# Attention into a gated MLP on one core: the order of work in the first six head pairs, the order of the weight loads, and the queue of the last stores

## The chip, the cores and the metric

The kernel runs on one core of a Trainium2 chip. A core has five engines with a queue each, which work on their own and meet only at semaphores: TensorE (PE in the profile; PEld is its loading of weights), VectorE (DVE), ScalarE (ACT), GpSimd (POOL) and SyncE (SP, which here only issues transfers). Each engine takes its instructions in the order in which the program issues them. The metric is device time in microseconds (us), lower is better. Before the change it is 472.25 us, the median of three runs from 472.16 to 472.7.

## The reference

The inputs are q, k and v of 8 batches, 12 heads, 448 positions and 64 columns, and two weight matrices. All is float32.

```python
scores = scale * np.matmul(q, k.transpose(0, 1, 3, 2))
m = np.max(scores, axis=-1, keepdims=True)
e = np.exp(scores - m)
attn = e / (np.sum(e, axis=-1, keepdims=True) + np.exp(-m) + 1e-09)
out = np.matmul(attn, v)          # -> x: (batch * position, head * column) = (3584, 768)
h = x @ w_in                      # (768, 2048)
g = h * np.tanh(np.where(h > 20.0, h, np.log1p(np.exp(np.minimum(h, 20.0)))))
result = g @ w_out                # (2048, 768) -> (3584, 768)
```

The scale is 1/8. The softmax has one more term in its denominator, exp(-m), and the activation g is Mish.

## The kernel before, in words

**Pairs.** Two heads of a batch are worked on together, as a pair; there are 48 pairs, six to a batch (`HP`), numbered p from 0. Of a pair, q, k and v are loaded by SP (line 144), cast to bf16 by POOL (lines 188, 194 and 174; pair 0 by DVE and ACT), and q and k are turned on PE by eight small transposes into one bank of PSUM (`transpose_pair`, line 211). `evac_qk` copies them from there to SBUF: q times the scale, and k, each 448 columns. In the first pairs both copies are ACT's (`act=True`, lines 242 and 252), later q is DVE's and k is ACT's. A bank for these transposes comes from a pool of two (`mo_take`), which is shared with two other uses below and is given back by the copy.

**Half steps.** A pair has four half steps s. I write (p, s). In s = 0, 1, 2 the scores of 128 rows of both heads are made by two matmuls (lines 282 and 285), in s = 3 the last 64 rows of both (lines 297 and 300). For each half step DVE takes the negated row maxima (line 308, 896 columns at once for s below 3, 448 for s = 3), and ACT the exponentials with their row sums (line 319, two instructions of 448 columns for s below 3, one for s = 3). After (p, 3) ACT also takes the exponential of the maxima (line 326). Three sets of banks hold scores, so the scores run three half steps ahead of the exponentials: `scores_ahead` issues the next ones as soon as `exps` has let a set go.

**Denominators and normalising.** `denominators` (lines 332 and 336) and `normalise` work on the pair before: a copy of the reciprocals (344), then seven multiplications, four on POOL (line 352) and three on DVE (354). The weights e are then turned. For pairs 0, 1 and 3 this is one transposing DMA from SP (line 358). For the others (`BY_PE`) it is four times seven transposes on PE (line 369), each followed by a copy of 896 columns on DVE (line 373). `av_pair` then makes the attention output, eight matmuls (line 391), and a copy to xT (line 400). These copies are put into a list, `late`, and issued by `flush_late` in the next half step, behind its exponentials; so they stand in the queue of their engine from that place on, whether or not the matmuls have come.

**The head of the program.** Before the loop, pairs 0 to 2 are loaded and pairs 0 and 1 turned. The loop over p from 0 to 5 (`HEAD`) and s from 0 to 3 then issues, in each half step: the exponentials of (p, s); in s = 1 the copies of q and k of pair p + 2; the late copies; the next scores; and in s = 0 the loads of pair p + 4, the denominators and the normalising of pair p - 1, the transposes of pair p + 2, the casts of pair p + 3 and some pieces of the weights. Three tables place the rest:

```python
TURN_HEAD = {(3, 2): [(2, 0)], (3, 3): [(2, 1)], (4, 0): [(2, 2)], (4, 1): [(2, 3)], ...}
AV_HEAD = {(3, 3): 0, (4, 2): 2, (4, 3): 1}
W_HEAD = {0: 3, 1: 1, 3: 1, 4: 1}
```

The first says at which half step which quarter of which pair's weights is turned on PE, the second where the attention outputs of pairs 0, 2 and 1 are made, the third how many pieces of weights are loaded for which p.

**The rest.** Units of three pairs follow. A unit u has twelve half steps, with matmuls of the layers as filler, and then eight groups of six matmuls of the first layer (line 414) with their Mish on ACT (line 420), each with its part of the work between units: denominators, normalising (for a unit's third pair wholly on POOL), transposes of the next pairs. The first unit in this form is u = 2, with pairs 6 to 8; pair 8 is still turned and copied inside its half steps, by DVE alone. Its first line 414 is the first large matmul of the program: it needs the outputs of pairs 0 to 5. The second layer (line 480) fills the half steps from u = 4 on. The weights come in 20 pieces, twelve of the first matrix and eight of the second, each one DMA from POOL (line 170). Six are loaded in the head, and `W_AT` and a line in the groups of u = 2 (718) place the others by half step.

**The end.** A block of 128 output rows is copied by DVE (line 467) and stored from SP (line 445), in as many parts as it crosses segments of 112 rows. The last block is stored in three column ranges, each in two parts of 112 and 16 rows.

Of the kernel before, what the change touches and what calls it, by code (L numbers as in the profile page):

```python
# [19 lines left out]
def kernel(  # L20
# [91 lines left out]
    GROUP_FROM = 2 * HP  # L112
    TURN_BY_DMA = (N_PAIRS - UNIT_PAIRS, N_PAIRS - UNIT_PAIRS + 1)
    q_rests = [
# [61 lines left out]
    def cast_pair(p, with_v=True):  # L176
# [10 lines left out]
        if p not in TURN_BY_DMA:  # L187
            cast_q(out=q_bf, in_=q_f.rearrange(by_t, t=NT))  # L188
        else:
            nc.gpsimd.tensor_scalar(  # L190
                out=q_bf, in0=q_f.rearrange(by_t, t=NT),
                scalar1=SCALE, scalar2=1.0, op0=ALU.mult, op1=ALU.mult,
            )
# [5 lines left out]
    def transpose_pair(p, bank=None):  # L199
# [16 lines left out]
        own = [] if bank is not None else [ps, ps_k] if p == 0 else [ps]  # L216
        qkT[p] = (by_s, own)

    def turn_by_dma(p):
        pair = [qk_pool.tile([128, S], BF16, tag=t, name=t) for t in ("qT", "kT")]  # L220
# [12 lines left out]
    def evac_qk(p, act=False):  # L233
        if p >= N_PAIRS:
            return
        (q_ps, k_ps), own = qkT[p]
        mo_free.extend(own)
        qT = qk_pool.tile([128, S], BF16, tag="qT", name="qT")
        kT = qk_pool.tile([128, S], BF16, tag="kT", name="kT")
        qkT[p] = (qT, kT)  # L240
# [193 lines left out]
    def store_rows(g, i, o_sb, cols):  # L434
# [6 lines left out]
        for r, n in sorted(parts, key=lambda part: -part[1]):  # L441
# [3 lines left out]
            nc.sync.dma_start(  # L445
# [126 lines left out]
    AV_HEAD = {(3, 3): 0, (4, 2): 2, (4, 3): 1}  # L572
# [3 lines left out]
    W_AT = ({5: 1, 9: 1}, {1: 1, 4: 1, 5: 1, 7: 1, 9: 1, 11: 1}, {3: 1, 5: 1, 7: 1, 9: 1})  # L576
# [15 lines left out]
    for p in range(HEAD):  # L592
        for s in range(STEPS):
# [20 lines left out]
            if (p, s) in AV_HEAD:  # L614
                av_pair(AV_HEAD[p, s], act=True)
# [3 lines left out]
    for u in range(UNITS_PER_B, N_UNITS + 2 * UNITS_PER_B):  # L619
# [86 lines left out]
        for f in range(FF_U):  # L706
# [11 lines left out]
            if u == UNITS_PER_B and f in (2, 6):  # L718
                load_w(1)
# [61 lines left out]
```

## Time and profile before

| | |
|---|---|
| median of three runs | 472.25 us |
| the profiled execution | 471.56 us |
| its span, first to last instruction | 469.7 us |
| busy PE / DVE / ACT / POOL | 93% / 72% / 73% / 40% of the span |
| first line 414 (first large matmul) | 63.61 us |
| last copy to the output buffer ends | 466.58 us |

The profile shows one execution. Its rows are groups of instructions by line, or single ones in order of time. In a row of the timeline stand the start, the duration, the engine, the line, the operation, output and input with their shapes, and in brackets how long the engine was idle before and what released it. PE's matmuls overlap in its pipeline, so that a row's duration is longer than its spacing from the next, and the same holds for ACT's and DVE's in small measure. A table by windows gives each engine's busy time in a stretch, the clock granted to TensorE as a share of the full one (PEclk), and the busy share of the transfer engines.

### The profile page before, as it was taken

How to read it: one execution, taken by the hardware profiler on the slowest of the kernel's cores; microseconds unless marked ns; L12 is line 12 of the kernel's file. 1: busy time of each engine (PE TensorE's matmuls, PEld its weight loads, DVE VectorE, ACT ScalarE, POOL GpSimd, SP SyncE). 2: the span in 40 equal slices, each digit the busy share in tenths (PEclk: the TensorE clock that was granted, in tenths of full speed). 3: DMA queues.
4: the chain of work that ended last, by engine and by line, in shares of the span. 5: the costliest groups of instructions: out<-in, count | busy, mean ns of one | idle time of the engine just before them, and what ended most of it. 6: DMA issues, size and time to landing. Idle time of an engine off the chain costs nothing.

```text
span 469.7 us, 8871 instructions
## 1 busy us (share of the span) xinstructions
PE 435.9 (93%) x3032; PEld 234.8 (50%) x3032; DVE 336.6 (72%) x727; ACT 344.2 (73%) x917; POOL 188.4 (40%) x358
## 2 busy tenths in 40 slices
PE   4565887899998999999999999999999999999996
PEld 2233544454544454555555454645455555555565
DVE  4788987968785897879787878788787978430121
ACT  5979787869796888979696969788797969312300
POOL 4876808364605354453636163435445360000000
PEclk9999698899999999999999999999999999999999
DMA  8999959999999989899999989998989995960213
GB/s 225 227 246 202 248 84 239 187 169 201 217 217 265 212 206 209 242 192 276 174 241 222 235 151 249 219 224 223 195 246 198 253 191 123 179 142 1 68 35 101
DMA packets 204300, 90.81 MB, mean 193 GB/s; under 512 B 160992, under 2 KB 200800, under 8 KB 204256
## 3 DMA queue, kind: packets, MB, share of 16 engines
q1 hardware_dynamic: 196768, 83.97, 82.5%
q0 software_dynamic: 7488, 6.29, 8.9%
q8 instruction: 23, 0.38, 0.3%
q14 instruction: 21, 0.17, 0.1%
HBM read 45.61 MB, written 11.01 MB: 121 GB/s over the span
## 4 chain that ended last, share of the span: by engine, by line
PE 79%; DVE 7%; ACT 7%; DMA 3%; issue 2%; POOL 2%; SPq 0%; DVEq 0%; ACTq 0%; POOLq 0%
PE mo L480 30%; PE mo L414 23%; PE b L391 6%; PE b L414 6%; ACT en L319 5%; DVE negm L308 5%; PE b L282 3%; PE sc L282 3%; PE sc L211 2%; PE mo L369 2%; PE b L211 1%; PE mo L290 1%; DMA q_f<-in_q_dram 1%; DMA w_in_sb<-in_moe_w_in_dram 1%; DMA k_f<-in_k_dram 1%
## 5 line engine op out<-in xcount | busy, mean ns | idle before, releaser
L480 PE MATMUL mo<-w_out_sb,gT 128*128 128x384 bf16 (+1 forms) x896 | 141.5, 304 | 0.7 <-DVE o_sb L467 0.7
L414 PE MATMUL mo<-xT,w_in_sb 128*128 128x448 bf16 x594 | 124.3, 352 | 1.2 <-DVE xT L400 0.6
L480 PEld LDWEIGHTS <-gT 128*128 128x128 bf16 x896 | 80.2, 98 | 58.5 <-issue 19.8
L420 ACT ACTIVATE gT<-mo 128x448 bf16<-128x448 f32 x99 | 53.7, 544 | 71.8 <-PE mo L414 71.5
L319 ACT ACTIVATE en<-sc,negm 128x448 bf16<-128x448 f32 x156 | 97.8, 641 | 11.5 <-DVE negm L308 8.2
L414 PEld LDWEIGHTS <-w_in_sb 128*128 128x128 bf16 x768 | 71.7, 98 | 65.6 <-issue 7.5
L308 DVE TENSOR_REDUCE negm<-b 128x1 f32<-128x448 f32 x144 | 79.7, 616 | 22.7 <-PE b L285 22.7
L308 DVE TENSOR_REDUCE negm<-sc 128x2 f32<-128x896 f32 x84 | 84.3, 1015 | 11.2 <-PE sc L285 4.0
L319 ACT ACTIVATE en<-b,negm 128x448 bf16<-128x448 f32 x144 | 89.5, 651 | 0.0
L352 POOL TENSOR_SCALAR en<-en,rden 128x448 bf16<-128x448 bf16 x115 | 71.8, 642 | 36.0 <-DVE rden L344 28.6
L188 POOL CAST q_bf<-q_f 112x512 bf16<-112x512 f32 x45 | 27.6, 614 | 105.1 <-DMA q_f<-in_q_dram 104.5
L467 DVE COPY o_sb<-mo 128x384 f32<-128x384 f32 (+1 forms) x64 | 32.2, 503 | 49.1 <-PE mo L480 45.3
L354 DVE TENSOR_SCALAR en<-en,rden 128x448 bf16<-128x448 bf16 x221 | 65.2, 363 | 0.5
L282 PE MATMUL sc<-kT,qT 64*128 64x448 bf16 x72 | 29.5, 418 | 12.7 <-ACT en L319 11.2
L414 PE MATMUL b<-xT,w_in_sb 128*128 128x448 bf16 x168 | 36.5, 352 | 0.0
L391 PE MATMUL b<-eT,v_bf 112*64 112x448 bf16 x304 | 35.8, 357 | 0.0
L319 ACT ACTIVATION_READ_ACCUMULATOR en<-sc,negm 128x1 f32 x156 | 33.0, 212 | 0.0
L319 ACT ACTIVATION_READ_ACCUMULATOR en<-b,negm 128x1 f32 x144 | 32.5, 226 | 0.0
L174 POOL CAST v_bf<-v_f 112x512 bf16<-112x512 f32 x48 | 29.7, 618 | 6.4 <-DMA v_f<-in_v_dram 5.9
L194 POOL CAST k_bf<-k_f 112x512 bf16<-112x512 f32 x47 | 28.8, 613 | 4.2 <-DMA k_f<-in_k_dram 3.7
L285 PE MATMUL sc<-kT,qT 64*128 64x448 bf16 x72 | 29.8, 422 | 0.0
L391 PEld LDWEIGHTS <-v_bf 112*64 112x64 bf16 x384 | 19.6, 111 | 19.0 <-issue 12.1
(67 smaller groups left out, 478.3 us busy)
## 6 DMA issues: line engine op xcount, KB each, us to landing
q_f<-in_q_dram SPq DMA_DIRECT2D x48, 224.0 KB, 4.7
k_f<-in_k_dram SPq DMA_DIRECT2D x48, 224.0 KB, 5.0
v_f<-in_v_dram SPq DMA_DIRECT2D x48, 224.0 KB, 5.1
w_in_sb<-in_moe_w_in_dram POOLq DMA_DIRECT2D x12, 256.0 KB, 6.1
w_out_sb<-in_moe_w_out_dram POOLq DMA_DIRECT2D x8, 384.0 KB, 6.7
out_dram<-o_sb SPq DMA_DIRECT2D x7, 336.0 KB, 3.3
out_dram<-o_sb SPq DMA_DIRECT2D x8, 288.0 KB, 4.2
out_dram<-o_sb SPq DMA_DIRECT2D x8, 240.0 KB, 3.5
```

Source lines behind the costliest of these rows:

```text
L174: nc.gpsimd.tensor_copy(out=casted[p][2], in_=loaded.pop(p)[2])
L282: nc.tensor.matmul(sc[0][:, 0:S], lhsT=qT[0:64, qa : qa + 128], rhs=kA, start=True, stop=True)
L285: nc.tensor.matmul(sc[1][:, 0:S], lhsT=qT[64:128, qb : qb + 128], rhs=kB, start=True, stop=True)
L308: nc.vector.tensor_reduce(out=negm, in_=scored, axis=AX.X, op=ALU.max, negate=True)
L319: nc.scalar.activation(out=st["en"][:, :, c, 0:SP_], in_=sc[bk][:, 0:S].rearrange("q (j c) -> q j c", j=NT), func=AF.Exp, bias=st["negm"][ ...
L352: nc.gpsimd.tensor_scalar(scalar2=1.0, op0=ALU.mult, op1=ALU.mult, **args)
L354: nc.vector.tensor_scalar(scalar2=None, op0=ALU.mult, **args)
L391: nc.tensor.matmul(av[h * 64 : (h + 1) * 64, 0:S], lhsT=v_bf[:, h, j * D : (j + 1) * D], rhs=e_h, start=(j == 0), stop=(j == NT - 1),)
L414: nc.tensor.matmul(h_ps[:, 0:S], lhsT=w_in_sb[:, dm, ff * 128 : (ff + 1) * 128], rhs=xT[b][:, dm, :], start=(dm == 0), stop=(dm == DM_T - 1),)
L420: nc.scalar.activation(out=gT[b][:, ff, :], in_=h_ps[:, 0:S], func=AF.Mish)
L467: nc.vector.tensor_copy(out=o_sb[:, cols], in_=st["o"][:, 0:n_cols])
L480: nc.tensor.matmul(st["o"][:, 0:n_cols], lhsT=src[:, ff, c0 : c0 + 128], rhs=w_out_sb[:, ff, cols], start=(ff == 0), stop=(ff == FF_T - 1),)
```

## The change

It has five parts.

1. For pairs 1 to 8 (`ONE_COPY`) POOL multiplies q by the scale in its cast, a multiplication in place of a copy, and q and k are copied from PSUM by one instruction of 896 columns, on ACT or, for pair 8, on DVE. The two buffers for q and k become one with two halves, for all pairs.
2. In the head, denominators and normalising of pair p - 1 are issued ahead of the scores of the half step instead of behind them, for p = 1 to 5, and the transposes of pair p + 2 too, for p = 1 to 4 (`TURN_FIRST`).
3. The attention output of pair 0 is made in (3, 1) instead of (3, 3). Its copy and that of pair 1 stay on ACT; pair 2's goes to DVE.
4. In the groups of u = 2 three pieces of weights are issued in the third group, instead of one there and one in the seventh. In the next unit the last place loads two pieces instead of one, and in the unit after two of four places fall away.
5. The smaller part of each of the last three stores is issued from ACT's queue.

```diff
+    ONE_COPY = range(1, HP + UNIT_PAIRS)
     TURN_BY_DMA = (N_PAIRS - UNIT_PAIRS, N_PAIRS - UNIT_PAIRS + 1)
+    SCALED_IN_CAST = (*ONE_COPY, *TURN_BY_DMA)
...
-        if p not in TURN_BY_DMA:
+        if p not in SCALED_IN_CAST:
             cast_q(out=q_bf, in_=q_f.rearrange(by_t, t=NT))
         else:
             nc.gpsimd.tensor_scalar(
...
+        if p in ONE_COPY:
+            by_s = ps[:, :].bitcast(BF16).rearrange("p (s n) -> p s n", s=2)[:, :, 0:S]
         qkT[p] = (by_s, own)
...
-        qT = qk_pool.tile([128, S], BF16, tag="qT", name="qT")
-        kT = qk_pool.tile([128, S], BF16, tag="kT", name="kT")
-        qkT[p] = (qT, kT)
+        qk = qk_pool.tile([128, 2, S], BF16, tag="qkT", name="qkT")
+        qT, kT = qkT[p] = qk[:, 0, :], qk[:, 1, :]
+        if p in ONE_COPY:
+            copy = nc.scalar.copy if act else nc.vector.tensor_copy
+            copy(out=qk, in_=by_s)
+            return
...
-        for r, n in sorted(parts, key=lambda part: -part[1]):
+        queues = [nc.sync, nc.scalar if (g, i) == (B // 2 - 1, 6) else nc.sync]
+        for queue, (r, n) in zip(queues, sorted(parts, key=lambda part: -part[1])):
...
-            nc.sync.dma_start(
+            queue.dma_start(
...
-    AV_HEAD = {(3, 3): 0, (4, 2): 2, (4, 3): 1}
+    TURN_FIRST = range(1, HEAD - 1)
+    AV_HEAD = {(3, 1): 0, (4, 2): 2, (4, 3): 1}
...
-    W_AT = ({5: 1, 9: 1}, {1: 1, 4: 1, 5: 1, 7: 1, 9: 1, 11: 1}, {3: 1, 5: 1, 7: 1, 9: 1})
+    W_AT = ({5: 1, 9: 1}, {1: 1, 4: 1, 5: 1, 7: 1, 9: 1, 11: 2}, {3: 1, 5: 1})
...
-            scores_ahead(HEAD * STEPS + 3)
             if s == (2 if p == HEAD - 1 else 0):
                 load_pair(p + 4)
+            if s == 0 and p:
+                denominators(att[p - 1])
+                normalise(p - 1, dma=p - 1 not in BY_PE, shared=BY_POOL)
+                if p in TURN_FIRST:
+                    transpose_pair(p + 2)
+            scores_ahead(HEAD * STEPS + 3)
             if s == 0:
-                if p:
-                    denominators(att[p - 1])
-                    normalise(p - 1, dma=p - 1 not in BY_PE, shared=BY_POOL)
+                if p and p not in TURN_FIRST:
                     transpose_pair(p + 2)
...
-                av_pair(AV_HEAD[p, s], act=True)
+                av_pair(AV_HEAD[p, s], act=AV_HEAD[p, s] != 2)
...
-            if u == UNITS_PER_B and f in (2, 6):
-                load_w(1)
+            if u == UNITS_PER_B and f == 2:
+                load_w(3)
```

More of the change, by code (lines that the diff above doesn't have):

```diff
@@ L216, in transpose_pair @@
         own = [] if bank is not None else [ps, ps_k] if p == 0 else [ps]
+        if p in ONE_COPY:
+            by_s = ps[:, :].bitcast(BF16).rearrange("p (s n) -> p s n", s=2)[:, :, 0:S]
         qkT[p] = (by_s, own)
     def turn_by_dma(p):
-        pair = [qk_pool.tile([128, S], BF16, tag=t, name=t) for t in ("qT", "kT")]
+        qk = qk_pool.tile([128, 2, S], BF16, tag="qkT", name="qkT")
+        pair = qk[:, 0, :], qk[:, 1, :]
         for dst, src in zip(pair, casted[p]):
@@ L235, in evac_qk @@
             return
-        (q_ps, k_ps), own = qkT[p]
+        by_s, own = qkT[p]
         mo_free.extend(own)
-        qT = qk_pool.tile([128, S], BF16, tag="qT", name="qT")
-        kT = qk_pool.tile([128, S], BF16, tag="kT", name="kT")
-        qkT[p] = (qT, kT)
+        qk = qk_pool.tile([128, 2, S], BF16, tag="qkT", name="qkT")
+        qT, kT = qkT[p] = qk[:, 0, :], qk[:, 1, :]
[3 more added lines that the diff above has]
+            return
+        q_ps, k_ps = by_s
         if act:
```

## The prediction

> **What bounds the kernel now.** I read the page first, then a table of busy time by stage, then the timeline of the early pairs, then the tail.
>
> ```profile
> span 469.7 us, 8871 instructions
> ```
> ```profile
> core 0: us, PE busy (x) PEld busy (x) DVE busy (x) ACT busy (x) POOL busy (x), PEclk, DMA share, GB/s
> 14.00:31.30 17.30, 9.21 (x51) 3.85 (x48) 14.97 (x30) 16.24 (x55) 14.65 (x23) 1.00 1.13 221
> 31.30:40.90 9.60, 7.75 (x67) 4.74 (x68) 8.36 (x16) 6.38 (x22) 6.61 (x12) 1.00 0.99 241
> 40.90:46.70 5.80, 2.59 (x24) 1.26 (x21) 4.11 (x9) 5.80 (x20) 3.62 (x7) 0.87 1.22 192
> 46.70:63.60 16.90, 13.98 (x108) 8.27 (x108) 16.64 (x29) 12.38 (x38) 11.37 (x19) 0.74 1.05 214
> 63.60:75.20 11.60, 11.59 (x79) 5.89 (x78) 8.17 (x24) 7.96 (x19) 2.77 (x5) 1.00 0.59 122
> 75.20:91.20 16.00, 12.22 (x101) 7.46 (x100) 14.28 (x21) 14.22 (x42) 11.66 (x19) 0.79 1.12 215
> 91.20:445.10 353.90, 351.59 (x2420) 185.85 (x2420) 258.17 (x578) 272.27 (x711) 131.11 (x259) 1.00 0.95 199
> ```
>
> Read the columns against the length of each stage. From 91.2 us to 445.1 us TensorE (PE) is busy 351.59 of 353.90 us, and the change leaves its work there alone. So what is done early can only shorten the stages ahead of the first large matmuls (63.6 us), and the tail. Those stages have three limits in turn: ScalarE (ACT) from 14.0 to 31.3 (16.24 of 17.30), nobody from 31.3 to 40.9 (VectorE, DVE, 8.36 and PE 7.75 of 9.60: a chain of waits), ACT again to 46.7 (5.80 of 5.80), and DVE from there to 63.6 (16.64 of 16.90). In the last of these an earlier start is kept but nothing is added to it.
>
> The second pair (p=1), from the timeline:
>
> ```profile
> 14.58 2.35 POOL L170 DMA_DIRECT2D w_in_sb<-in_moe_w_in_dram  x3
> 15.49 0.53 PE L297 MATMUL sc<-kT,qT 64*64 64x448 bf16 x1 [0.77 <-ACT en L319]
> 15.96 0.62 ACT L319 ACTIVATE en<-sc,negm 128x448 bf16<-128x448 f32 x1
> 16.00 0.56 PE L211 MATMUL mo<-ident,q_bf 112*128 112x112 bf16 x4
> 16.35 0.58 PE L211 MATMUL mo<-ident,k_bf 112*128 112x112 bf16 x4
> 16.75 0.15 DVE L332 SCALAR_TENSOR_TENSOR den<-sums,expm 128x7 f32<-128x7 f32 x1
> 17.04 0.54 ACT L242 ACTIVATE qT<-mo 128x448 bf16<-128x448 bf16 x1 [0.36 <-PE mo L211]
> 17.48 0.53 ACT L252 COPY kT<-mo 128x448 bf16<-128x448 bf16 x1
> 17.54 2.80 POOL L352 TENSOR_SCALAR en<-en,rden 128x448 bf16<-128x448 bf16 x4 [0.61 <-DVE rden L344]
> 17.89 0.65 ACT L319 ACTIVATE en<-sc,negm 128x448 bf16<-128x448 f32 x1
> 17.99 1.08 DVE L308 TENSOR_REDUCE negm<-sc 128x2 f32<-128x896 f32 x1
> 20.86 0.60 POOL L194 CAST k_bf<-k_f 112x512 bf16<-112x512 f32 x1
> ```
>
> ACT's second exponential of the half step would let the next operation start about 16.57, yet the copy of q starts at 17.04. It waits for the transposes (to 16.93), which stand on PE behind the scores at 15.49, which waited 0.77 for ACT. ACT loses 0.47 us in this pair by an order on PE alone.
>
> The fourth to sixth pairs:
>
> ```profile
> 20.37 4.34 SPq L358 DMA_TRANSPOSE eT<-en  x1
> 26.82 0.63 ACT L319 ACTIVATE en<-sc,negm 128x448 bf16<-128x448 f32 x1
> 30.77 0.53 PE L282 MATMUL sc<-kT,qT 64*128 64x448 bf16 x1 [1.87 <-ACT en L319]
> 33.65 1.55 PE L391 MATMUL mo<-eT,v_bf 112*64 112x448 bf16 x8
> 35.25 0.53 ACT L400 CAST xT<-mo 128x448 bf16<-128x448 f32 x1 [2.59 <-PE mo L391]
> 35.68 0.64 ACT L319 ACTIVATE en<-sc,negm 128x448 bf16<-128x448 f32 x1
> 40.64 0.95 PE L391 MATMUL mo<-eT,v_bf 112*64 112x448 bf16 x8
> 42.52 0.66 ACT L319 ACTIVATE en<-sc,negm 128x448 bf16<-128x448 f32 x1
> 46.70 1.09 DVE L308 TENSOR_REDUCE negm<-sc 128x2 f32<-128x896 f32 x1 [0.78 <-ACT expm L326]
> ```
> ```profile
> DMA to landing us min/median/max: 8.6/8.6/8.6
> ```
>
> The largest stall of the head is at 35.25: ACT stood 2.59 us because the copy of the first attention output sat in its queue while PE, at its matmuls from 33.65, was late. The last line is the landing time of the transfer issued at 20.37 (pair 0's transpose by DMA).
>
> **The change part by part.** All times are on the clock of the profile before.
>
> *Pair 0.* Pairs 1 and 2 get one copy of 896 columns instead of two of 448. Two cost 0.85 today (17.04 to 17.89). No such copy on ACT is in the trace. Ends: 0.61, what DVE takes for 896 bf16 columns out of PSUM (first row below), and 0.85, no gain. I take 0.76: the step from 21 to 448 columns on ACT costs 0.53 - 0.225 = 0.305 us (second row below), the doubling costs about as much again, 0.32, on the 0.44 by which the two copies stand apart.
>
> ```profile
> L373 DVE COPY eT<-mo 112x896 bf16<-112x896 bf16 x20 | 12.1, 610 | 0.0
> L329 ACT ACTIVATE expm<-negm 128x21 f32<-128x21 f32 x14 | 3.1, 225 | 0.0
> L190 POOL TENSOR_SCALAR q_bf<-q_f x2: 616/619/622, 367.8 to 372.3; 112x512 bf16<-112x512 f32 x2
> ```
>
> Gain 0.09 a pair; 0.15 for the two. (The Trainium skill, "ScalarE: Activation LUTs", section "What ACT_TABLE_LOAD costs", gives 186 ns plus 0.833 ns per element for an ACTIVATE with immediate operands and an overlap of 93 ns back to back; by that an estimate for one copy of 896 is 0.84 us. By it the merge saves next to nothing, and the total below would be about 0.2 us higher, 470.2.) The scaling moves from the copy into GpSimd's (POOL's) cast: 0.619 us by the L190 row against 0.60 for the plain cast of k at 20.86, so 0.02 a pair, hidden as long as POOL is not what the transposes wait for (pair 2, below). Pair 8's two copies on DVE become one of 0.61; two of the DVE's small copies take about that, so nothing.
>
> *Pair 1.* Transposes go ahead of the scores, behind scores that end before 15 us; the casts they need are older. The wait of 0.47 goes and the copy saves 0.09: 0.56.
>
> *Denominators first.* DVE does den to the last normalisation in 16.75 to 17.99, 1.24 us, ahead of a narrow reduction instead of behind it. The reduction comes 1.24 later, and ACT needs it only two half steps on, at its last exponential of the pair, so this costs nothing. If the cover goes, the price is what remains of 1.24. What it brings is POOL's normalisation sooner, but in pair 1 POOL is held until 14.58 + 2.35 = 16.93 by the three weight issues, so 17.54 becomes about 16.95, and the end, with 2.80, 19.75.
>
> *Pair 2.* What is late next is POOL: the casts of pair 4 follow the normalisation; k ends today at 20.86 + 0.60, then about 20.9. The transposes need 0.93 (16.00 to 16.93) and end at 21.9, where ACT would take them at 21.6. So 0.3 of the 0.56 is lost, PE's scores behind the transposes are late by as much, covered by DVE's 1.24; gain 0.2. Together the exponentials of half step (3, 1) move from 26.82 to 25.9.
>
> *First attention output two half steps sooner.* Its operand lands: issue 19.8 plus 8.6, 28.4. PE reaches it near 27.8, after the scores that follow those exponentials, in the gap of 1.87 us that the row at 30.77 shows, and does it in 1.55, to 29.95. It is queued ahead of the scores of (4, 1), which then begin at 30.0 and not 30.77. Its copy on ACT now stands behind the exponentials of (3, 2), which end at 25.9 + 1.24 + 0.76 + 1.24 = 29.15. ACT waits 0.85 there, so the exponentials of (4, 0) come at 30.0 + 0.44 + 0.62 and about 0.1 for a small one, 31.1; those of (4, 1) follow at 32.4 instead of 35.68: 3.3 us won.
>
> *Pair 4.* Then DVE is what is late, and PE behind it. From the wide reduction of (4, 1) at 30.6 DVE has three wide reductions (1.08 by the row at 17.99), four copies of pair 2's transposes (0.61), the 1.24 and a narrow reduction, half as wide, 0.55: 7.5 us, to 38.1. PE can then do the outputs of pairs 2 and 1, 0.95 each by the row at 40.64, with the scores of a half step between them, 0.33 (0.53 at 30.77, shortened as 0.95 is to 1.55): 40.3. ACT's copy of the second, 0.44, ends at 40.8; exponentials (5, 1) start there, against 42.52. So 1.7 of the 3.3 remains. Were PE still as slow as at 33.65 (1.55 and 0.53), it would be 42.2, and 0.3 would remain. I take the fast value: the output at 28.4 fills PE's gap, and the slow matmuls of today end after a busy stretch like the one that then starts there. The copy of pair 2's output goes from ACT to DVE, 0.61; behind it stands the reduction of (5, 2), which ACT needs a half step later, so nothing. From 42.52 to DVE's reduction at 46.70 are 4.18 us today; with one merged copy in them and scores at the fast value, 44.8. Gain 1.9. As DVE is full to 63.6, it is still 1.9 at the first large matmul and at the end of the span.
>
> *Weight pieces.* Rows of POOL's issues:
>
> ```profile
> 58.38 1.43 POOL L170 DMA_DIRECT2D w_in_sb<-in_moe_w_in_dram  x2
> 72.43 4.32 POOL L352 TENSOR_SCALAR en<-en,rden 128x448 bf16<-128x448 bf16 x7 [12.62 <-DVE rden L344]
> 76.70 0.75 POOL L170 DMA_DIRECT2D w_in_sb<-in_moe_w_in_dram  x1
> ```
>
> Two more issues behind those at 58.38 cost POOL 1.5 us in 12.62 us of idle time; the transfers meet a DMA share of 0.59 in 63.6 to 75.2. The issue at 76.70, ahead of casts, goes. The doubled issue later and the two fewer at the end shift 0.75 us each on a queue that waits for loads. Nothing, unless that cover is gone: 1.5 us.
>
> *The tail.*
>
> ```profile
> 466.60 0.79 SPq L445 DMA_DIRECT2D out_dram<-o_sb  x2
> L445 SPq DMA_DIRECT2D out_dram<-o_sb x2: 317/371/425, 466.6 to 467.0; - x2
> DMA to landing us min/median/max: 1.6/1.6/1.7
> ```
>
> The last two stores are issued one behind the other on SP, the second 0.47 (0.79 - 0.317) after the first. On ACT's queue, idle then, it goes out with the first: the last landing moves from 466.60 + 0.47 + 1.6 to 466.60 + 1.7, 0.37, say 0.4. No store was issued from ACT in the trace; ends 0 and 0.47.
>
> *Sum.* 1.9 + 0.4 = 2.3 us. The profiled execution took 471.56 us, 469.7 of it span, and is 0.69 below the median of 472.25. A difference carries over: 472.25 - 2.3 = 469.95, 470.0.
>
> **The rivals.**
>
> *More is won (467.2 to 469.0).* DVE's idle time from 14.0 to 46.7 is 2.33 + 1.24 + 1.69 = 5.26 us. If all but the added 0.61 were closed and the tail gave 0.4, the time would be 467.2. For it: DVE is the one engine that is full until 63.6. Against it: the landing of 8.6 us. If that were 0.8 less, ACT's wait of 0.85 would go: 469.2.
>
> *The head's gain is lost again (471.6 to 472.1).* The output matmuls stand on PE ahead of the scores of (4, 1). Each us by which the transfer lands after 28.4 goes straight into PE, ACT and DVE; with a landing at 30.3, the 1.9 us are gone and 471.85 remains. PE at its slow value in pair 4 would give nearly the same, 471.5. Against the first: the issue would have to come as late as 20.37 with a landing of 9.9 in place of 8.6.
>
> *Slower: the clock.* PE's granted clock was 0.74 in 46.7 to 63.6 and 0.79 in 75.2 to 91.2: if that is full and half clock alone, 8.8 and 6.7 us at half. Both spells lie where DVE or a mixture sets the pace. PE alone sets it in 63.6 to 75.2, now at 1.00. If the shorter, differently spaced head put a spell of 6.7 us there, it would cost half, 3.4: 470.0 + 3.4 = 473.4. It decides from 4.6 us at half clock on. (The Trainium skill, "TensorE: Matmul & The Clock Gate", Part 1 on the HAM clock gate, says that a free-running window of about 3.4 us decides and that an idle one halves the clock. By it a shift of 2 us can move a spell by a window; the trace agrees with the two levels and shows no spell in this stage.) Against it: PE is busy 13.98 of 16.90 ahead of the stage and its clock had come back before it.
>
> **How the numbers follow.** Forecast 0.55 (its own range 469.0 to 471.2: the tail's ends, 0.09 a pair for the copy, 0.8 of landing either way), more 0.15, lost 0.12, slower by the clock 0.13, slower by anything else (POOL's casts late in every pair, a price for the second queue) 0.05. About 0.2% (0.94 us) is what can be told from no change here. Faster 0.70, same 0.12, slower 0.18. The range that leaves 2 in 10 out goes from 468.0, inside the first rival, to 472.8, inside the last.
>
> **What would show it.** In the profile after: no wait of ACT's copy of q and k for transposes in half steps (1, 1) and (3, 1), and a small one in (2, 1), with PE released by POOL's cast; one ACT copy of 896 columns near 0.76; the first L391 starting near 28.4 rather than 33.65 and released by a DMA; ACT's wait before its copy near 0.85 rather than 2.59; exponentials (4, 1) near 32.4; the first L414 near 61.7; the last store's issue from ACT beside SP's. The prediction is wrong if the first L414 stands where it was, if it moves but the stages behind it lengthen, or if the granted clock falls below 1.00 in the first eight L414 groups.

## The result, and the profile after

The changed kernel takes 470.02 us, the median of 13 runs from 467.87 to 471.88; the kernel before, on the same chip, 472.7 (13 runs). The ratio is 0.9941, with a 95% interval from 0.9919 to 0.9962: faster by 0.6%. Unaltered and run twice more (e1 and e12), each time beside the kernel before, it gave 0.9975 [0.9955, 0.9995] and 0.9948 [0.9924, 0.9972]. The mean of the three differences of medians is (2.68 + 0.99 + 1.93) / 3 = 1.9 us; 2.3 had been forecast. But the time did not come from where the forecast took it.

The profiled execution took 471.50 us, near the slow end of its runs. Its page begins:

```profile
span 469.7 us, 8842 instructions
```

The same seven stages as in the prediction, by the clock of this execution:

```profile
core 0: us, PE busy (x) PEld busy (x) DVE busy (x) ACT busy (x) POOL busy (x), PEclk, DMA share, GB/s
14.00:31.30 17.30, 8.38 (x46) 3.59 (x45) 16.80 (x26) 13.27 (x41) 12.09 (x19) 1.00 1.04 210
31.30:40.90 9.60, 8.25 (x62) 4.80 (x61) 9.39 (x19) 8.54 (x26) 8.08 (x13) 1.00 1.12 211
40.90:46.70 5.80, 2.73 (x24) 1.27 (x24) 5.73 (x12) 5.05 (x15) 4.18 (x8) 0.99 1.23 258
46.70:63.60 16.90, 14.41 (x96) 8.44 (x97) 15.51 (x27) 11.90 (x38) 13.27 (x22) 0.60 1.05 220
63.60:75.20 11.60, 11.60 (x86) 5.90 (x82) 8.56 (x25) 8.64 (x22) 1.12 (x2) 1.00 0.83 143
75.20:91.20 16.00, 12.77 (x100) 7.59 (x100) 13.71 (x19) 13.24 (x37) 13.39 (x22) 0.79 1.08 210
91.20:445.10 353.90, 352.24 (x2433) 186.66 (x2428) 262.76 (x581) 274.28 (x717) 130.29 (x257) 1.00 0.94 198
```

From 14.0 to 31.3 ScalarE, which was the limit there, does 2.97 us less work (13.27 in place of 16.24), and VectorE is busy 16.80 of 17.30. The rows of the timeline say why:

```profile
14.84 2.34 POOL L172 DMA_DIRECT2D w_in_sb<-in_moe_w_in_dram  x3
16.35 0.91 ACT L247 COPY qkT<-mo 128x896 bf16<-128x896 bf16 x1
16.42 0.17 DVE L353 COPY rden<-rden 128x7 f32<-128x7 f32 x1
16.50 5.29 DVE L363 TENSOR_SCALAR en<-en,rden 128x448 bf16<-128x448 bf16 x3
17.13 0.66 ACT L328 ACTIVATE en<-sc,negm 128x448 bf16<-128x448 f32 x1
17.22 2.49 POOL L361 TENSOR_SCALAR en<-en,rden 128x448 bf16<-128x448 bf16 x4
19.69 0.61 POOL L192 TENSOR_SCALAR q_bf<-q_f 112x512 bf16<-112x512 f32 x1
20.25 0.60 POOL L196 CAST k_bf<-k_f 112x512 bf16<-112x512 f32 x1
20.81 0.60 POOL L176 CAST v_bf<-v_f 112x512 bf16<-112x512 f32 x1
21.36 0.76 POOL L172 DMA_DIRECT2D w_in_sb<-in_moe_w_in_dram  x1
22.35 0.64 ACT L328 ACTIVATE en<-sc,negm 128x448 bf16<-128x448 f32 x1 [3.85 <-DVE negm L317]
...
31.68 1.71 PE L400 MATMUL mo<-eT,v_bf 112*64 112x448 bf16 x8
33.42 0.53 ACT L409 CAST xT<-mo 128x448 bf16<-128x448 f32 x1 [0.24 <-PE mo L400]
65.37 1.31 PE L423 MATMUL mo<-xT,w_in_sb 128*128 128x448 bf16 x6
```

The copy of 896 columns stands directly behind an exponential, as forecast. Then VectorE's three normalising multiplies take 5.29 us. The group of line 363 in the stretch from 14 to 32 us shows that it is one of them:

```profile
L363 DVE TENSOR_SCALAR en<-en,rden x9: 318/331/4799, 16.5 to 31.7; 128x448 bf16<-128x448 bf16 x9
```

The median is 331 ns, the longest 4799. GpSimd meanwhile goes from its weight issues to its own four multiplies, its three casts and the next weight issue without a gap, and VectorE comes through where the casts end. ScalarE then waits 3.85 us for the row maxima that are queued behind VectorE's multiplies. So the first large matmul stands at 65.37, later than before (63.61), and this execution still has the span of the one before. What it lost up to there, it won behind it: 469.7 - 65.37 = 404.3 us, against 469.7 - 63.61 = 406.1.

The experiments ask three things: what the long multiply is and how often it costs, what the early attention output is worth, and where the 1.8 us behind the first large matmul come from. This table has, of one profile each, where pair 0's transposing transfer lands (its issue and its time to landing added), the length of the head (from ScalarE's first exponential, which starts at 7.5 to 8.1 us, to the first large matmul), and what follows the head (the span less the start of the first large matmul). The kernels ran on three chips (e1 to e4, e5 to e9, e10 to e13), each beside the kernel before, so medians of different groups are best compared by their ratios.

| kernel | pair 0's transfer lands | head | behind it |
|---|---|---|---|
| before | 20.37 + 8.6 = 29.0 | 55.65 | 406.1 |
| order alone (e3) | 19.86 + 9.5 = 29.4 | 55.38 | 406.6 |
| last stores alone (e4) | 20.24 + 10.4 = 30.6 | 56.30 | 405.6 |
| weight pieces alone (e6) | 20.07 + 11.8 = 31.9 | 56.97 | 404.4 |
| early output alone (e7) | 20.81 + 11.3 = 32.1 | 57.91 | 405.3 |
| changed | 21.85 + 7.8 = 29.7 | 57.51 | 404.3 |
| changed, again (e1) | 19.82 + 9.5 = 29.3 | 53.78 | 405.2 |
| changed, again (e12) | 20.59 + 11.0 = 31.6 | 56.38 | 404.4 |
| VectorE first (e5) | 19.81 + 9.2 = 29.0 | 53.24 | 404.4 |
| VectorE first, again (e13) | 20.34 + 11.2 = 31.5 | 56.74 | 404.1 |
| VectorE first, late output (e10) | 20.44 + 11.2 = 31.6 | 55.48 | 405.0 |
| VectorE first, pieces later (e11) | 20.37 + 7.3 = 27.7 | 54.30 | 404.3 |
| pieces moved to pairs 1 and 2 (e2) | 19.67 + 10.7 = 30.4 | 60.46 | 404.2 |
| the same, VectorE first (e9) | 20.11 + 9.8 = 29.9 | 62.46 | 404.3 |

### The profile page after: what moved, and what is told of

It is laid out like the page before. It is cut to its first block, busy times and chain, and to the rows that moved or that the text cites. A ratio compares the mean times of both kernels' runs of the same rounds, so it can differ in the third digit from the quotient of the medians.

```text
span 469.7 us, 8842 instructions
## 1 busy us (share of the span) xinstructions
PE 437.2 (93%) x3032; PEld 235.7 (50%) x3032; DVE 344.3 (73%) x727; ACT 344.0 (73%) x909; POOL 189.1 (40%) x358
## 4 chain that ended last, share of the span: by engine, by line
PE 79%; DVE 10%; ACT 6%; issue 2%; DMA 1%; SPq 0%; POOL 0%; DVEq 0%; POOLq 0%
PE mo L490 30%; PE mo L423 22%; DVE negm L317 7%; PE b L400 6%; PE b L423 6%; ACT en L328 5%; PE b L291 3%; PE sc L291 3%; PE mo L378 2%; PE sc L213 2%; PE b L213 1%; PE mo L299 1%; DVE en L363 1%; PE mo L400 1%; DVE eT L382 1%
## 5 line engine op out<-in xcount | busy, mean ns | idle before, releaser
L490 PEld LDWEIGHTS <-gT 128*128 128x128 bf16 x896 | 80.2, 98 | 58.5 <-issue 19.8
L363 DVE TENSOR_SCALAR en<-en,rden 128x448 bf16<-128x448 bf16 x221 | 72.0, 395 | 0.5
L190 POOL CAST q_bf<-q_f 112x512 bf16<-112x512 f32 x37 | 22.7, 614 | 94.8 <-DMA q_f<-in_q_dram 94.1
L291 PE MATMUL sc<-qkT 64*128 64x448 bf16 x72 | 29.7, 420 | 15.5 <-ACT en L328 14.9
L196 POOL CAST k_bf<-k_f 112x512 bf16<-112x512 f32 x47 | 29.4, 626 | 6.5 <-DMA k_f<-in_k_dram 5.9
L294 PE MATMUL sc<-qkT 64*128 64x448 bf16 x72 | 30.0, 425 | 0.0
```

The source lines that it names most:

```text
L291: nc.tensor.matmul(sc[0][:, 0:S], lhsT=qT[0:64, qa : qa + 128], rhs=kA, start=True, stop=True)
L294: nc.tensor.matmul(sc[1][:, 0:S], lhsT=qT[64:128, qb : qb + 128], rhs=kB, start=True, stop=True)
L363: nc.vector.tensor_scalar(scalar2=None, op0=ALU.mult, **args)
L490: nc.tensor.matmul(st["o"][:, 0:n_cols], lhsT=src[:, ff, c0 : c0 + 128], rhs=w_out_sb[:, ff, cols], start=(ff == 0), stop=(ff == FF_T - 1),)
```

## The experiments

**e1, the changed kernel again.** No edit.

> The changed kernel once more, unaltered. Its first profile shows the second of pair 0's three normalisations on VectorE taking 4.80 us (16.74 to 21.54) while GpSimd works without a gap. Theory A, GpSimd: the normalisation starts while GpSimd is still issuing the first three weight pieces and gets in only when GpSimd's queue has a gap; then this row is again between 4 and 5 us in this profile, and the time is 468 to 472. Theory B, a rare event of that one execution: the row is 0.33 us, the first large matmul stands near 61.6 instead of 65.3, and the time is near 466.

471.52 us (10 runs, 468.79 to 472.89), ratio 0.9975 [0.9955, 0.9995]. Its profile is the one at 468.79. In the timeline:

```profile
14.50 2.34 POOL L172 DMA_DIRECT2D w_in_sb<-in_moe_w_in_dram  x3
16.70 0.82 DVE L363 TENSOR_SCALAR en<-en,rden 128x448 bf16<-128x448 bf16 x3
17.04 2.76 POOL L361 TENSOR_SCALAR en<-en,rden 128x448 bf16<-128x448 bf16 x4 [0.20 <-DVE rden L353]
29.40 1.70 PE L400 MATMUL mo<-eT,v_bf 112*64 112x448 bf16 x8 [1.49 <-DMA eT<-en]
31.14 0.53 ACT L409 CAST xT<-mo 128x448 bf16<-128x448 f32 x1 [1.80 <-PE mo L400]
40.64 0.53 ACT L409 CAST xT<-mo 128x448 bf16<-128x448 f32 x1 [0.75 <-PE mo L400]
61.83 1.41 PE L423 MATMUL mo<-xT,w_in_sb 128*128 128x448 bf16 x6 [0.58 <-DVE xT L409]
```

The same program, without the long multiply: the weight issues end at 16.84, GpSimd idles 0.20 us for the reciprocals, and VectorE's three take 0.82. In the first profile they ended at 17.18, after the reciprocals at 16.59, and GpSimd never idled. The issues end a third of a microsecond apart in the two executions. The first large matmul is at 61.83, where 61.7 had been forecast. The short multiply is what theory B expected, a matter of one execution; its time, near 466, did not come.

**e2, the pieces out of the way.** The weight issues ahead of GpSimd's first multiplies go to pairs 1 and 2.

```diff
-    W_HEAD = {0: 3, 1: 1, 3: 1, 4: 1}
+    W_HEAD = {1: 2, 2: 2, 3: 1, 4: 1}
```

> The changed kernel with the weight pieces of the head placed later: none at p = 0, two at p = 1 and two at p = 2, one each at 3 and 4. Theory A: GpSimd is idle when the first normalisation comes, the three take 0.8 to 1.2 us together instead of 5.29, ACT's wait of 3.85 us at 22.35 is gone, the first large matmul comes near 61.6, and the time is 465.5 to 467. Theory B: nothing changes, 468 to 472.

474.7 us (12 runs), ratio 1.0048 [1.0028, 1.0068]: slower, which neither theory had. From the timeline:

```profile
21.30 1.62 POOL L172 DMA_DIRECT2D w_in_sb<-in_moe_w_in_dram  x2
22.01 5.26 DVE L363 TENSOR_SCALAR en<-en,rden 128x448 bf16<-128x448 bf16 x3
22.95 2.49 POOL L361 TENSOR_SCALAR en<-en,rden 128x448 bf16<-128x448 bf16 x4
27.34 10.41 SPq L367 DMA_TRANSPOSE eT<-en  x1
45.19 1.71 PE L400 MATMUL mo<-eT,v_bf 112*64 112x448 bf16 x8 [2.53 <-DMA eT<-en]
```

In pair 0 the multiplies are short; in pair 1, where the issues now stand ahead of GpSimd's multiplies, they take 5.26 us. The long multiply moved with the issues. The last two rows show a second cost, of which e9 tells.

**e3, the order alone,** and **e4, the last stores alone,** on the kernel before.

```diff
+    TURN_FIRST = range(1, HEAD - 1)
...
-            scores_ahead(HEAD * STEPS + 3)
...
+            if s == 0 and p:
+                denominators(att[p - 1])
+                normalise(p - 1, dma=p - 1 not in BY_PE, shared=BY_POOL)
+                if p in TURN_FIRST:
+                    transpose_pair(p + 2)
+            scores_ahead(HEAD * STEPS + 3)
             if s == 0:
-                if p:
-                    denominators(att[p - 1])
-                    normalise(p - 1, dma=p - 1 not in BY_PE, shared=BY_POOL)
+                if p and p not in TURN_FIRST:
                     transpose_pair(p + 2)
```

> The kernel before with one part of the change: denominators, normalising and transposes ahead of the scores. Theory A: this part alone brings the stall (a normalisation of 4 to 5 us), because it moves the normalisations from 17.25 to before 16.93, where GpSimd issues weights; the first large matmul comes 2 to 4 us later than 63.6 and the time is 474 to 476. Theory B: no stall, 0.5 to 1.0 us faster than before.

471.11 us (10 runs), 0.9984 [0.9960, 1.0008]. No multiply is long in its profile, as theory B had it. The head is 55.38, 0.27 shorter than before's: in this profile the order alone shortens the head by next to nothing.

```diff
-        for r, n in sorted(parts, key=lambda part: -part[1]):
+        queues = [nc.sync, nc.scalar if (g, i) == (B // 2 - 1, 6) else nc.sync]
+        for queue, (r, n) in zip(queues, sorted(parts, key=lambda part: -part[1])):
...
-            nc.sync.dma_start(
+            queue.dma_start(
```

> The kernel before with only the smaller part of the last stores on ACT's queue. The prediction's term: 0.4 us faster. In the changed kernel's profile the span ends 3.27 us after the last copy to the output buffer ends, and in the profile before 3.12 us; by that reading 0 to 0.2 us slower.

471.93 us (12 runs), 0.9983 [0.9961, 1.0006]. Neither e3 nor e4 can be told from no change. In e4's profile 3.24 us lie between the end of the last copy to the output buffer and the end of the span; before, 3.17 (from the unrounded times in the traces; the views give the span to 0.1 us). In the ten profiles with two queues it is 3.23 to 3.25, in the four with one 3.16 to 3.18: the two queues bring nothing, and cost about 0.07.

**e5, VectorE's multiplies first.** GpSimd's four wait for a copy of the reciprocals. If that copy is issued behind VectorE's three, GpSimd's queue must pause for them.

```diff
-            nc.vector.tensor_copy(out=st["rden2"], in_=st["rden"])
-        for i in range(NTILE):
+            if on_pool:
+                nc.vector.tensor_copy(out=st["rden2"], in_=st["rden"])
+        for i in (*range(shared, NTILE), *range(shared)):
+            if shared and i == 0:
+                nc.vector.tensor_copy(out=st["rden2"], in_=st["rden"])
```

> The changed kernel, but in each normalisation shared with GpSimd, VectorE's three normalising multiplies are issued ahead of the copy of the reciprocals that GpSimd's four wait for. GpSimd's queue must then pause until VectorE is through. Theory A (GpSimd keeps VectorE's multiplies out as long as its queue has no gap): no profile shows the three multiplies of pair 0 taking 5.29 us, they take 0.8 to 1.3; GpSimd's four begin 0.5 to 0.8 later than 17.0; the first large matmul begins at 61.5 to 63.0, and the time is 467.5 to 469.5, with a spread of the runs under 3 us against 4.0 of the changed kernel. Theory B (the 4.8 us were a wait for something else, the reciprocals or a buffer): the long multiply appears as before in some executions, the median stays at 470.0 and the spread at 4 us. Theory C (the stall is avoided, but GpSimd's later start costs as much): no long multiply, first large matmul at 63.5 or later, time 470.5 to 472.

468.92 us (6 runs, 467.11 to 471.06), 0.9922 [0.9894, 0.9951]. The three multiplies take 0.83, 0.98 and 0.89 us in the first three pairs, GpSimd's four start at 17.30, and the first large matmul is at 60.86, a little sooner than theory A's 61.5 to 63.0. The time is as theory A has it. The spread is not: 4 us, where under 3 was expected. So the long multiply alone is not what spreads the runs, as far as six runs can say.

**e9, e2 with VectorE's multiplies first.** The edit is that of e2 and that of e5 together. The weight issues stay where the long multiply was.

> The kernel in which the first weight pieces are issued in pairs 1 and 2 instead of pair 0 (it took 474.7, with a multiply of pair 1 taking 5.26 us), and VectorE's three multiplies ahead of the copy that GpSimd waits for. The weight issues stand where they stood, directly ahead of GpSimd's multiplies. Theory A (a GpSimd queue without a gap keeps VectorE out): the three multiplies of pair 1 take 0.8 to 1.3 us, the first large matmul begins at 61.5 to 64 in place of 68.6, the time is 468 to 470.5. Theory B (the weight issues themselves are what costs VectorE and the kernel the time, whatever the order of the copy): it stays at 473 to 475.

476.51 us (5 runs), 1.0087 [1.0059, 1.0115]. From the timeline, and from the view of the transfer from 25 to 30 us:

```profile
22.06 1.38 DVE L366 TENSOR_SCALAR en<-en,rden 128x448 bf16<-128x448 bf16 x3
26.54 15.17 SPq L370 DMA_TRANSPOSE eT<-en  x1
27.83 1.48 POOL L172 DMA_DIRECT2D w_in_sb<-in_moe_w_in_dram  x2
47.72 0.63 ACT L328 ACTIVATE en<-sc,negm 128x448 bf16<-128x448 f32 x1 [9.54 <-DMA eT<-en]
```
```profile
DMA to landing us min/median/max: 21.1/21.1/21.1
```

The long multiply is gone (1.38 for 5.26), although the weight issues stand where they stood: what held it was GpSimd's own work starting straight behind the issues, not the issues. The time got worse all the same, so theory A fails on the time: pair 1's transposing transfer now stands between four weight pieces and occupies SP's queue for 15.17 us, and lands after 21.1. ScalarE waits 9.54 us for it. In e2 the same transfer took 17.8 (10.41 on the queue), where e5's took 9.4 (5.76). So e2 was not slower by the long multiply alone. Which engine of the transfer path gives way to which is not shown.

**e6, the weight pieces alone,** part 4 of the change on the kernel before.

> The kernel before with the later weight pieces alone (three issues at once in place of two single ones ahead of the first feed-forward unit, two in one half step, two fewer at the end). The prediction gave this part nothing: 472.3 +- 0.5, and TensorE's idle time from 130 to 160 us, 1.94 in the profile of before, stays at 1.5 to 2.1. The rival: this part is where the changed kernel's smaller idle time there comes from (0.91 and 0.01 us in its two profiles): idle time under 1.0, time 470.8 to 471.8.

470.65 us (10 runs), 0.9964 [0.9944, 0.9984]. This is the rival, even 0.15 below its range: the part that the prediction gave nothing is worth 1.5 us. In the timeline of the kernel before:

```profile
145.94 0.61 POOL L188 CAST q_bf<-q_f 112x512 bf16<-112x512 f32 x1 [4.03 <-DMA q_f<-in_q_dram]
146.62 0.37 PE L211 MATMUL sc<-ident,q_bf 112*128 112x112 bf16 x4 [0.51 <-POOL q_bf L188]
147.17 0.37 PE L211 MATMUL b<-ident,k_bf 112*128 112x112 bf16 x4 [0.19 <-POOL k_bf L194]
150.18 0.37 PE L211 MATMUL sc<-ident,q_bf 112*128 112x112 bf16 x4 [0.36 <-POOL q_bf L188]
150.73 0.37 PE L211 MATMUL b<-ident,k_bf 112*128 112x112 bf16 x4 [0.19 <-POOL k_bf L194]
```

and with the pieces alone:

```profile
143.72 0.61 POOL L188 CAST q_bf<-q_f 112x512 bf16<-112x512 f32 x1 [3.43 <-DMA q_f<-in_q_dram]
147.00 0.36 PE L211 MATMUL sc<-ident,q_bf 112*128 112x112 bf16 x4 [0.18 <-DVE qT L244]
```

TensorE's waits for GpSimd's casts (0.51 + 0.19 + 0.36 + 0.19 = 1.25 us) are gone. The casts waited for loads of q, and these come earlier. Why they do stands in SP's queue, before and with the pieces alone:

```profile
120.63 15.63 SPq L358 DMA_TRANSPOSE eT<-en  x3
```
```profile
121.34 12.92 SPq L358 DMA_TRANSPOSE eT<-en  x3
```

Three transposing transfers stand there ahead of the loads. Before, two more pieces are issued just ahead of them (117.50 to 118.99; with the pieces alone the last is issued by 117.3), and the first of the three occupies the queue for 6.22 us; with the pieces alone, for 4.08. It is 6.22 to 6.61 in the four kernels without this part of the change and 4.07 to 4.21 in the ten with it. So SP comes to the loads sooner, at 134.32 in place of 136.31. TensorE's idle time from 130 to 160 falls from 1.94 to 0.90, and what follows the head from 406.1 to 404.4. So about 1.0 of these 1.7 us is traced to the loads; the rest is not. By the table, it is 404.1 to 405.2 in the ten kernels with these pieces and 405.3 to 406.6 in the four without; the means are 404.5 and 405.9, a gain of 1.4 us.

**e7, the early output alone.** On the kernel before, pair 0's output at (3, 1) and pair 2's copy on VectorE.

```diff
-    AV_HEAD = {(3, 3): 0, (4, 2): 2, (4, 3): 1}
+    AV_HEAD = {(3, 1): 0, (4, 2): 2, (4, 3): 1}
...
-                av_pair(AV_HEAD[p, s], act=True)
+                av_pair(AV_HEAD[p, s], act=AV_HEAD[p, s] != 2)
```

> The kernel before with the first attention output at half step (3, 1) and the copy of the output of pair 2 on VectorE, nothing else: the scores still ahead of the transposes, the denominators behind, two copies. By the prediction's working the transfer lands at 29 (20.37 + 8.6) and the output is queued ahead of the scores: the exponentials of (4, 1) at 33.0 to 33.5 in place of 35.68, but VectorE's late work of pair 4 then limits: first large matmul at 62.0 to 62.6, time 470.8 to 471.5. Rival (the order of the first pairs is the part that matters and the output alone only moves the wait): first large matmul at 63.3 to 64, time 472 to 473.

471.65 us (10 runs), 0.9985 [0.9963, 1.0008]; first large matmul at 65.78. Its output matmuls waited 3.35 us for the transfer, which was issued at 20.81 and landed 11.3 later, not 8.6. Neither theory had 65.78 (62.0 to 62.6, or 63.3 to 64): theory A had left the landing at 8.6.

**e10, the early output undone; e11, fewer pieces ahead of the transfer; e12 and e13, the changed kernel and e5 beside them on one chip.** The edits against e5:

```diff
# e10
-    AV_HEAD = {(3, 1): 0, (4, 2): 2, (4, 3): 1}
+    AV_HEAD = {(3, 3): 0, (4, 2): 2, (4, 3): 1}
# e11
-    W_HEAD = {0: 3, 1: 1, 3: 1, 4: 1}
+    W_HEAD = {0: 2, 3: 2, 4: 1, 5: 1}
```

> The kernel with VectorE's multiplies first, but the first attention output back at half step (3, 3), its copy still on ScalarE. From the first exponential to the first large matmul the profiles so far have 55.65 us (before), 55.38 (the order alone), 57.91 (the early output alone), 53.78 (the changed kernel without the stall) and 53.24 (VectorE first). Theory A (the early output pays, but only once the order lets the transposing transfer start by 19.8): this span grows by 1.0 to 2.0, to 54.3 to 55.3, and the time by as much, 469.9 to 470.9 against 468.9. Rival (the early output pays nothing even then, the order and the one copy give it all): 53.0 to 53.6 and the same time within 0.4 us.

> The kernel with VectorE's multiplies first, and of the six weight pieces of the first pairs two issued in pair 0, none in pair 1, two in pair 3 and one each in pairs 4 and 5 (before: 3, 1, 0, 1, 1). Theory A (weight pieces in flight are what stretches the transposing transfers): pair 0's takes at most 9.0 us from its issue to the output's start (9.28 with the earlier pieces), pair 1's occupies its queue under 5.2 us (5.76), from the first exponential to the first large matmul 52.3 to 53.1, time 467.5 to 468.8. Rival (what stretches them is other traffic, or the two pieces of pair 3 stretch pair 3's own transfer as the two of pair 2 did): 53.3 to 56, time 469 to 472, with the wait at the output of pair 1 or 3.

> The changed kernel, unaltered, on the same chip as the kernel with VectorE first. By theory A on the stall it is 470.0 to 471.5 and 0.8 to 2.0 slower than that kernel; its profile has either the three multiplies of pair 0 at over 4 us and a first large matmul at 64.5 or later, or the three at 0.8 to 1.3 us and 61.5 to 63. The rival, that the order of the copy changes nothing in the mean: both within 0.5 us.

> The kernel with VectorE's three multiplies ahead of the copy that GpSimd waits for, as before (468.92), beside the changed kernel on one chip: 468.3 to 469.5, no multiply group of VectorE above 1.5 us in the first four pairs, and the first large matmul 53.0 to 53.8 after the first exponential. The rival as for the changed kernel beside it: the same time within 0.5 us.

| | median (runs) | ratio to before |
|---|---|---|
| e10, late output | 470.35 (7) | 0.9931 [0.9906, 0.9955] |
| e11, pieces later | 468.95 (6) | 0.9910 [0.9878, 0.9943] |
| e12, changed kernel | 470.85 (12) | 0.9948 [0.9924, 0.9972] |
| e13, VectorE first | 470.66 (9) | 0.9935 [0.9903, 0.9968] |

e12 and e13 are within 0.2 us of each other: the rival was right, in the mean the order of the copy changes nothing that these runs can tell. Theory A, by which e12 is 0.8 to 2.0 slower and e13 takes 468.3 to 469.5 with a head of 53.0 to 53.8, was not. (e5, which is the same kernel as e13, had 468.92 on another chip.) The long multiply is in two profiles (changed, e2) of the five with this order of work and the copy first (also e1, e3 and e12), and in none of the five with VectorE first. So it was seen, and avoided, but over many executions it is not what sets the time. A row of e12 from the timeline, and of e11:

```profile
31.64 1.70 PE L400 MATMUL mo<-eT,v_bf 112*64 112x448 bf16 x8 [2.96 <-DMA eT<-en]
33.38 0.53 ACT L409 CAST xT<-mo 128x448 bf16<-128x448 f32 x1 [3.26 <-PE mo L400]
64.25 1.41 PE L423 MATMUL mo<-xT,w_in_sb 128*128 128x448 bf16 x6 [0.58 <-DVE xT L409]
```
```profile
28.07 1.71 PE L403 MATMUL mo<-eT,v_bf 112*64 112x448 bf16 x8
29.82 0.53 ACT L412 CAST xT<-mo 128x448 bf16<-128x448 f32 x1 [0.26 <-PE mo L403]
47.65 0.63 ACT L328 ACTIVATE en<-sc,negm 128x448 bf16<-128x448 f32 x1 [1.45 <-DVE den L341]
62.17 1.41 PE L426 MATMUL mo<-xT,w_in_sb 128*128 128x448 bf16 x6 [0.58 <-DVE xT L412]
```

In e12 the matmuls are queued and wait 2.96 us for the landing, with the scores behind them; ScalarE waits 3.26. In e11, with two pieces of weights in pair 0 and none in pair 1, the transfer lands after 7.3 us and nothing waits for it.

So the early output is a bet on the landing. Read the table above by it. With the whole order and the output early, the head is 53.51 (mean of e1 and e5) where the transfer lands at 29.0 to 29.3, and 56.56 (mean of e12 and e13) where it lands at 31.5 to 31.6. Counted from each profile's first exponential, the landing is 2.25 us later in the second two, and so is ScalarE's copy of the output (25.51 and 25.29, against 23.09 and 23.21). The other 0.8 us of the 3.05 arise behind that copy, most of them in e13, where the granted clock from 46.7 to 63.6 is 0.51 (0.83 in e5, 0.81 in e1, 0.72 in e12). That the clock makes them is not shown. With the output late it is 55.38 at 29.4 (e3, with two copies) and 55.48 at 31.6 (e10), and the landing does not matter. The early output wins about 1.9 in the first case and loses about 1.1 in the second, by one or two profiles each. So theory A of e10 is half right: the late output's 55.48 was close to its upper end of 55.3, but on this chip the early output beside it was longer still, and the medians were the same within 0.4 us (470.35 and 470.66), as the rival said.

Of e11's numbers the landing came as theory A had it (7.3 us, under 9.0); the queue time of pair 1's transfer (5.72, not under 5.2), the head (54.30, not 52.3 to 53.1) and, by 0.15, the time did not. The head is in the rival's range, the time between the two. Pair 3's transfer, with the two pieces ahead of it, occupies its queue for 7.11 us (4.95 in e5, but 6.99 in e10 too), and nothing in the head waits for it. With the wait at the output gone, ScalarE's wait for VectorE at 47.65 is what is late next. e11's ratio of 0.9910 and e5's 0.9922 are the lowest; their intervals overlap those of the changed kernel, so that they beat the kernel before is shown, and that they beat the changed one is not.

## Why the prediction was right

The time was right, 470.0 against 470.02, as was the sign. The agreement is luck: two errors of about the same size made it, a head term that holds in only some executions, and a term of the weights that was missed. By its own sign of being wrong, that the first large matmul stands where it was (63.61), the mechanism failed in two of the changed kernel's three profiles (65.37 and 64.25) and came in one (61.83).

- **Copy of 896 columns.** The row at 16.35 lasts 0.91, and the next exponential starts 0.78 behind it, where 0.76 had been taken. That is worth 0.85 - 0.78 = 0.07 a pair. (The working's 0.15 for two pairs is 0.18 by its own 0.09.) (The estimate of 0.84 by the Trainium skill, "ScalarE: Activation LUTs", section "What ACT_TABLE_LOAD costs", was 0.06 above what the trace shows.)
- **The wait for the transposes** of 0.47 in pair 1 is gone, as forecast.
- **"Denominators first costs nothing."** This step failed in the profiled execution. What was queued behind VectorE's multiplies was named and its cover was judged right, but what stands beside them on GpSimd was not looked at. The price was "what remains of 1.24 if the cover goes"; it was 3.85 us of ScalarE's time.
- **Landing and first output.** With the clean profile e1: issue 19.82 (19.8 forecast), output matmuls at 29.40 (28.4), ScalarE's wait 1.80 (0.85). The 0.95 are those of the landing, 9.5 in place of 8.6. The 8.6 was one row of one execution; the fourteen profiles have 7.3 to 11.8. In e12 it was 11.0, and the second rival ("lost": each us by which the transfer lands late goes straight into PE, ACT and DVE) describes it, at one us per us of landing as far as ScalarE's copy.
- **Pair 4, bounded by VectorE.** Second copy on ScalarE 40.64 to about 41.1 in e1 (end forecast at 40.8), first large matmul 61.83 (61.7). Right: the 0.95 of landing was swallowed here, as VectorE's work is late anyway. In e11, with an early landing, VectorE is what is waited for as well.
- **Head, 1.9 us.** In e1 55.65 - 53.78 = 1.9. In the profile after it is -1.9, in e12 -0.7. The mean of the changed kernel's three heads, 55.89, is 0.4 below the mean of the three profiles with the old order of the head (before, e4, e6: 56.31). These lie 3.7 and 1.3 us apart among themselves, so 0.4 cannot be told from nothing. The term was right for its landing, and too large as a mean.
- **Weight pieces, "Nothing".** The step that failed most: 1.4 us. The working looked at GpSimd's time for the issues and at the stage they move to. It said that two issues fewer at the end "shift 0.75 us each on a queue that waits for loads", and did not ask what the loads themselves gain when the pieces are out of the way, nor looked for TensorE's waits between 130 and 160 us, or at the transposing transfers that stand on SP's queue ahead of those loads.
- **Tail, 0.4.** Measured nothing. The second store went out with the first (466.5, both), but from the end of the last copy to the end of the span it is 3.25 us after and 3.17 before. The issues of the last stores in the profile after, with the last column the time to landing:

```profile
out_dram<-o_sb SPq DMA_DIRECT2D x1, 84.0 KB, 1.8
out_dram<-o_sb ACTq DMA_DIRECT2D x1, 12.0 KB, 1.9
```

  The working put the second store 0.47 behind the first; it was 0.36, as the second issue is the one that takes 0.425 (0.79 - 0.425). And what the earlier issue saves, the landing loses: the second store landed 1.57 us after its issue before, and 1.93 after, beside the first. The last landing comes 1.95 us behind the last copy before, and 1.96 after. (The Trainium skill, "DMA: Bandwidth & Descriptors", section "Rules for kernel authors", says that spreading transfers over issuing engines only saves issue time; the trace agrees, with 0.36 saved at the issue and nothing at the end.)
- **Sum.** 1.9 + 0.4 forecast, and a mean of 1.9 found in the medians. The weight pieces alone gave 1.5 (e6), with an interval (0.9944 to 0.9984) that holds 0.9955, the mean of the whole change's three ratios; what the other four parts add to them is not shown to differ from nothing.
- **Slower by the clock.** Did not come: PEclk is 1.00 from 63.6 to 75.2 after, and 0.79 from 75.2 to 91.2 as before. From 46.7 to 63.6 it is 0.60 after and 0.74 before; the working gave that stage to VectorE, and what the clock costs there no run separates.

## What to carry to other kernels

A landing time that a step hangs on should be read as a range over several transfers and executions, not as the one row at hand: work queued ahead of other work to catch a transfer pays if the transfer is early, and costs every engine behind it if it is late. Where two engines share a job, look at what the other one does next to the part that is moved, and whether the two will now work at the same moment. And of pieces that are loaded sooner, ask which later transfers and loads then come sooner too, not only where the issues fit.

## What the runs showed of the hardware

- **A multiply of VectorE held for 4.8 us by GpSimd's work.** 4799 ns where the median is 331, over seven instructions of GpSimd (17.22 to 21.41) that do not depend on it; in e2 4774 ns, again to the end of the third cast. By the trace neither multiply waits for a semaphore, so, other than the opening says, these two engines do not meet only at semaphores. It is gone where GpSimd's queue pauses ahead of its multiplies (0.20 us in e1, 0.97 in e5). (The Trainium skill, "SBUF — State Buffer", section "Who interferes with whom", has a port pair of VectorE and GpSimd that is an exclusive lock, whoever comes first, for an instruction. The trace agrees that VectorE is held as a whole, and goes further: it was not let in between GpSimd's instructions, up to the end of the third cast.) That it is this lock, no run shows. Nor is a GpSimd queue without a gap enough: in e12 GpSimd goes from its issues to its multiplies with 0.04 us between, as in the first profile, but VectorE's three have ended by 17.43, ahead of GpSimd's first at 18.08, and none is held. In e12's next pair they do meet, and the multiply takes 0.88 us, not 4.8. What decides between a short and a long hold stays open.
- **The same transposing transfer took 7.3 to 11.8 us to land.** In the ten profiles with three pieces issued in pair 0 and no long multiply, it lands by 29.4 where GpSimd's first piece is issued by 14.58 (before, e1, e3, e5), and at 30.6 or later where that is at 14.88 or later (e4, e6, e7, e10, e12, e13). That issue stands behind casts that each wait 0.2 to 0.3 us for their load. So a slower start of the loads goes with a later landing; e11's 7.3 says that the weight pieces in flight matter as well. It is one profile, and what makes the loads faster or slower from one execution to the next stays open.
- **Four weight pieces around a transposing transfer stretched it to 21.1 us** (e9; 17.8 in e2), and its time on SP's queue from about 5 to 15.17. Two pieces more, issued just ahead of a later transposing transfer, took it from 4.07 to 4.21 us on that queue (ten profiles) to 6.22 to 6.61 (four).
